# Projecting q once and spreading its rows through a DRAM scratch, in an attention kernel that feeds a gated feed-forward block

## The chip, the cores and the metric

The kernel runs on one core of a Trainium2 chip. A core has five engines with instruction streams of their own: TensorE (PE in the profile, with its weight loads as PEld), VectorE (DVE), ScalarE (ACT), GpSimd (POOL) and SyncE (SP), which here only issues DMA transfers. They meet through semaphores. The metric is the device time of one execution in microseconds (us). The profile is of one execution; its span runs from the first to the last instruction that it records.

## The reference

There are two blocks, in fp32. The first is attention with a polynomial sketch: every row of q and of k, 32 numbers long, is projected by S1 and S2 to 8 numbers each, and the outer product of the two results, 64 numbers, is its feature vector.

```python
def phi(x):                                   # x: (4, 4, 1088, 32)
    a = np.einsum('rd,bhsd->bhsr', S1, x)
    b = np.einsum('rd,bhsd->bhsr', S2, x)
    return np.einsum('bhsi,bhsj->bhsij', a, b).reshape(*x.shape[:-1], r * r)   # r = 8
q_p, k_p = phi(q), phi(k)
kv  = np.einsum('bhsf,bhsd->bhfd', k_p, v)
z   = np.sum(k_p, axis=2)
num = np.einsum('bhsf,bhfd->bhsd', q_p, kv)
den = np.einsum('bhsf,bhf->bhs', q_p, z)[..., None] + 1e-06
attn = num / den                              # then x = (4*1088, 4*32) = (4352, 128)
gate = 1.0 / (1.0 + np.exp(-(x @ w_gate)))    # w_gate, w_val: (128, 1536)
out  = (gate * (x @ w_val)) @ w_out           # w_out: (1536, 128)
```

The three weight matrices and S1, S2 arrive as 64-bit floats, so the kernel narrows them to fp32 itself with integer operations.

## The kernel before, in words

**The feed-forward block.** The 4352 tokens are cut into nine chunks, eight of 512 and one of 256. `xT` holds the tokens transposed. For a chunk the 1536 columns of the weights are taken in twelve blocks of 128. One *wave* (`w1`, matmuls at L293) computes gate and value of one block into a PSUM tile of the pool `psm`, which has two buffers; ACT takes the sigmoid of one half (L301, tile `sg`); `glu` (L311, VectorE) multiplies it by the other half and frees the PSUM tile; `w2` (L253) multiplies the result by the block of w_out and sums over the twelve blocks in the tile `moeout`. There are 102 waves.

**The attention block** handles one batch at a time, in two halves of q (n=0 with 512 rows of a head, n=1 with 576). `kps` (L379) projects k onto compact features, eight matmuls of 64 rows with the outputs of S1 and S2 of four heads side by side; VectorE transposes them (L389, `kab`), and `outer` (L400) forms the 64 features on POOL, or on VectorE for batch 0. `sum_z` (POOL, L494 to L499) sums them over the rows. `kv` (L460, L472) multiplies by v, `ndt` (L505) transposes. For q the feature dimension must lie on the partitions, so `ab` (L423) multiplies q twice by weights that already repeat the rows of S1 (`aps`) and of S2 (`bps`); ACT copies the first out (L433, `asb`), and VectorE multiplies the two (L442) into `qp`. An `r_group` is one such step: the second operand of one pair of heads together with the first operand of the next. Then `den` (L525) and `num` (L560) multiply `qp` by z and by kv; `invert` and `divide` on VectorE (L536 to L570) write the quotient into `xT`.

**What sets the order.** The order on PE, VectorE, ACT and POOL is written out by hand; each engine executes its instructions in that order. `slot(group, waves)` issues one piece of the attention of a batch and then some waves, each with the pending `glu` and `w2` in front of it. A wave is only issued if the attention has delivered its tokens. Only the DMA issues on SP may be moved by the scheduler; they too are executed in order.

**Narrowing.** In chunk 0 every wave also narrows weights: block j goes through four steps over several waves, POOL and ACT at first (L95, L99), then VectorE (L103, L107), then ACT and POOL (L111, L112), last VectorE (L115), which writes the fp32 block that the next wave uses. `load_w` fetches the 64-bit weights.

Of the kernel before, what the change touches and what calls it, by code (L numbers as in the profile page):

```python
# [8 lines left out]
F32 = mybir.dt.float32  # L9
# [5 lines left out]
MUL = ALU.mult  # L15

P = 128
# [3 lines left out]
def kernel(  # L21
# [12 lines left out]
    nc = tc.nc  # L34

    B, H, S, D = q.shape
    R = S1.shape[0]
# [6 lines left out]
    T = S // 32  # L44
# [7 lines left out]
    const = ctx.enter_context(tc.tile_pool(name="const", bufs=1))  # L52
    ld = ctx.enter_context(tc.tile_pool(name="ld", bufs=2))
    sbA = ctx.enter_context(tc.tile_pool(name="sbA", bufs=2))
    raw = ctx.enter_context(tc.tile_pool(name="raw", bufs=4))
    sbN = ctx.enter_context(tc.tile_pool(name="sbN", bufs=1))
    sbG = ctx.enter_context(tc.tile_pool(name="sbG", bufs=6))

    psm = ctx.enter_context(tc.tile_pool(name="psm", bufs=2, space=bass.MemoryType.PSUM))
    pso = ctx.enter_context(tc.tile_pool(name="pso", bufs=1, space=bass.MemoryType.PSUM))  # L60
    ps2 = ctx.enter_context(tc.tile_pool(name="ps2", bufs=1, space=bass.MemoryType.PSUM))
# [11 lines left out]
    TP = T // 2  # L73
    q_chk = [(0, 8), (8, TP - 8)]
# [245 lines left out]
    def glu():  # L320
        if moe["gate"] is not None:
            moe["gate"]()
            moe["gate"] = None
# [48 lines left out]
    KP, QP, ND, KAB, ASB, KVZ, KVD, RB = {}, {}, {}, {}, {}, {}, {}, {}  # L372

    def kps(b):
        t = ps2.tile([P, 2, 512], F32, tag="two", name="kps")
# [19 lines left out]
    def outer(b, pi, m0, m1, j0=0, j1=NJK, eng=nc.gpsimd):  # L395
# [8 lines left out]
            op=MUL,  # L404
        )

    def ab(a_of=None, b_of=None, pool_b=None):

        mm = []
        if a_of is not None:  # L410
            aps = psm.tile([P, 2, 512], F32, tag="wave", name="aps")
            mm.append((a_of, aps, sa))
        if b_of is not None:
            pool, tag = (ps2, "two") if pool_b is None else pool_b
            bps = pool.tile([P, 2, 512], F32, tag=tag, name="bps")
            mm.append((b_of, bps, sb))
        for c in range(2):
            for m in range(2):
                for (bb, pr, n), dst, sx in mm:
                    h = 2 * pr + m  # L420
                    rows = slice(32 * h, 32 * h + 32)
                    t0, tn = q_chk[n]
                    nc.tensor.matmul(  # L423
                        out=dst[64 * c : 64 * c + 64, m, : 32 * tn],
                        lhsT=sx[rows, :],
                        rhs=qT_of[bb][rows, t0 : t0 + tn, c, :],
                        start=True,
                        stop=True,
                    )
        if a_of is not None:  # L430
            w = 32 * q_chk[a_of[2]][1]
            ASB[a_of] = sbA.tile([P, 2, 288], F32, tag="asb", name="asb", bufs=3)
            nc.scalar.copy(out=ASB[a_of][:, :, :w], in_=aps[:, :, :w])  # L433
        if b_of is not None:

            def mult():
                bb, pr, n = b_of
                if bb not in QP:
                    QP[bb] = sbA.tile([P, H, TP * 32], F32, tag="qp", name="qp")
                t0, tn = q_chk[n]  # L440
                w = 32 * tn
                nc.vector.tensor_tensor(  # L442
                    out=QP[bb][:, 2 * pr : 2 * pr + 2, 32 * t0 : 32 * t0 + w],
                    in0=bps[:, :, :w],
                    in1=ASB[b_of][:, :, :w],
                    op=MUL,
                )

            return mult

    def kv(b, j_list, zsum=None):

# [67 lines left out]
    def den(b, n):  # L520
        t0, tn = q_chk[n]
        w = 32 * tn
        dps = ps1.tile([P, 512], F32, tag="one", name="dps")
        for h in range(H):
            nc.tensor.matmul(  # L525
                out=dps[32 * h : 32 * h + 32, :w],
                lhsT=zb[b % 2][:, h, :],
                rhs=QP[b][:, h, 32 * t0 : 32 * t0 + w],
                start=True,
                stop=True,  # L530
            )

        def invert():

            dT = sbA.tile([P, 9, 32], F32, tag="dT", name="dT")
            nc.vector.transpose(out=dT[:, :tn].rearrange("p t c -> p (t c)"), in_=dps[:, :w])  # L536
            rc = sbA.tile([P, 9, 2], F32, tag="rc", name="rc")
            nc.vector.tensor_scalar_add(rc[:, :tn], dT[:, :tn, :2], 1e-6)
            nc.vector.reciprocal(out=rc[:, :tn], in_=rc[:, :tn])

            rb = sbA.tile([P, 9, 2, 32], F32, tag="rb", name="rb")
            r0 = rc[:, :tn]
            nc.vector.transpose(
                out=rb[:, :tn].rearrange("p t c s -> p (t c s)"),
                in_=bass.AP(
                    tensor=r0.tensor, offset=r0.offset, ap=[list(r0.ap[0]), [1, 2 * tn], [0, 32]]
                ),
            )
# [106 lines left out]
    outer(1, 0, 0, 1)  # L655
    slot(lambda: r_group((1, 0, 0), None), 1)
    outer(1, 0, 1, 2)

    for b in range(1, B):
        more = b + 1 < B  # L660
# [5 lines left out]
        if b == 1:  # L666
            outer(b, 1, 0, 1)
        slot(lambda: r_group((b, 0, 1), (b, 1, 0)), wn)
        if b == 1:
            outer(b, 1, 1, 2)  # L670
# [11 lines left out]
        slot(lambda: den(b, 0)(), wn)  # L682

        def num0_den1():
            divide = num(b, 0)
            invert = den(b, 1)
            divide()
            invert()

        slot(num0_den1, wn)  # L690
        slot(lambda: num(b, 1)(), 1)
    slot(None, 10**3)


# [28 lines left out]
```

## Time and profile before

| | |
|---|---|
| time, median of 8 runs | 325.9 us (325.17 to 327.23) |
| the profiled execution | 325.5 us, of which its span is 323.7 us |
| granted TensorE clock | 0.998 of full speed |
| PE busy, 1562 matmul records | 311.5 us |
| VectorE, ACT, POOL busy | 141.4, 86.0, 48.5 us |
| DMA | 14.08 MB |

Every fp32 matmul shows as two records, so a wave has four. Ends of matmuls are modelled and consecutive ones overlap; the distance from start to start tells what one costs. In the lists of instructions the square bracket gives the idle time before an instruction and what ended it. SPq is the DMA queue of SyncE.

### The profile page before, as it was taken

To read this page: it belongs to the slowest core of one execution; us is meant where nothing else is said; L and a number is where in the kernel's file an instruction comes from. 1 tells how busy PE (TensorE), PEld (TensorE's weight loads), DVE (VectorE), ACT (ScalarE), POOL (GpSimd) and SP (SyncE) were. 2 spreads that over 40 slices of the span, in tenths; PEclk is the share of its full clock that TensorE was granted. 3 is DMA by queue.
4 is the path that set the end of the run, shared out by engine and by line. 5 is a ranking of instruction groups with operands and counts; after the bars stand their busy time and mean duration, and the time that the engine had idled before them with its cause. 6 is when DMAs were issued, how large, how long until landed. Compare 5 with 4: busy or idle time off the path is not lost.

```text
span 323.7 us, 3953 instructions
## 1 busy us (share of the span) xinstructions
PE 311.5 (96%) x1562; PEld 136.7 (42%) x1562; DVE 141.4 (44%) x248; ACT 86.0 (27%) x156; POOL 48.5 (15%) x53
## 2 busy tenths in 40 slices
PE   7779999899999999999999999999999999999995
PEld 2423433433344443333454434444444444444684
DVE  4887998455534333653313543242223222322321
ACT  2534544231233122122322221222222222222220
POOL 1433456674000290000000000000000000000000
PEclk9999999999999999999999999999999999999999
DMA  7999222130000200001000200010002000200021
GB/s 185 356 311 327 50 72 70 52 55 2 0 0 2 32 0 2 0 4 31 0 2 0 33 2 0 1 24 9 0 0 34 0 0 0 32 0 0 2 32 16
DMA packets 25586, 14.08 MB, mean 43 GB/s; under 512 B 19168, under 2 KB 22752, under 8 KB 25568
## 3 DMA queue, kind: packets, MB, share of 16 engines
q1 hardware_dynamic: 24736, 13.44, 15.9%
q10 hardware_dynamic: 832, 0.39, 0.6%
q8 instruction: 12, 0.20, 0.3%
q14 instruction: 6, 0.05, 0.1%
HBM read 11.60 MB, written 2.23 MB: 43 GB/s over the span
## 4 chain that ended last, share of the span: by engine, by line
PE 86%; DVE 4%; POOL 4%; DMA 3%; ACT 1%; issue 1%; SPq 0%; POOLq 0%; ACTq 0%; DVEq 0%
PE wave L293 52%; PE moeout L253 27%; DMA w_in<-in_moe_w_out_dram 2%; DMA k<-in_k_dram 1%; PE nps L560 1%; PE aps L423 1%; PE dps L525 1%; DVE w_sb L115 1%; POOL head L112 1%; DVE head L107 1%; POOL kp L400 1%; PE kvz L460 1%; POOL z L494 1%; PE bps L423 1%; PE kps L379 1%
## 5 line engine op out<-in xcount | busy, mean ns | idle before, releaser
L293 PE MATMUL wave<-xT,w_sb 128*128 128x512 f32 (+1 forms) x432 | 191.8, 570 | 3.4 <-DVE g L311 1.8
L311 DVE TENSOR_TENSOR g<-wave,sg 128x512 f32<-128x512 f32 x102 | 69.8, 685 | 122.3 <-ACT sg L301 122.0
L293 PEld LDWEIGHTS wave<-xT,w_sb 128*128 128x128 f32 x432 | 80.9, 190 | 99.0 <-issue 83.9
L301 ACT ACTIVATE sg<-wave 128x512 f32<-128x512 f32 x102 | 60.9, 597 | 213.1 <-PE wave L293 213.1
L253 PE MATMUL moeout<-g,w_sb 128*128 128x512 f32 (+1 forms) x216 | 105.9, 583 | 0.0
L253 PEld LDWEIGHTS moeout<-g,w_sb 128*128 128x128 f32 x216 | 38.2, 189 | 43.2 <-issue 38.7
L442 DVE TENSOR_TENSOR qp<-bps,asb 128x512 f32<-128x512 f32 (+1 forms) x16 | 11.5, 720 | 19.9 <-PE bps L423 14.6
L400 POOL TENSOR_TENSOR kp<-kab 128x576 f32<-128x576 f32 (+1 forms) x8 | 13.6, 1712 | 39.2 <-DVE kab L389 39.2
L112 POOL TENSOR_TENSOR head<-head,tail 128x384 int32<-128x384 int32 (+1 forms) x13 | 12.3, 947 | 24.3 <-DVE head L107 15.6
L423 PE MATMUL bps<-qT,s 32*64 32x256 f32 (+1 forms) x128 | 11.0, 412 | 0.4 <-DVE kab L389 0.4
L423 PE MATMUL aps<-qT,s 32*64 32x256 f32 (+1 forms) x128 | 11.3, 413 | 0.0
L433 ACT COPY asb<-aps 128x512 f32<-128x512 f32 (+1 forms) x16 | 9.7, 608 | 3.3 <-PE aps L423 1.9
L115 DVE SCALAR_TENSOR_TENSOR w_sb<-cap,head 128x384 f32<-128x384 f32 x12 | 9.8, 817 | 1.8 <-POOL head L112 1.8
L570 DVE TENSOR_TENSOR xT<-nps,rb 128x512 f32<-128x512 f32 (+1 forms) x8 | 5.8, 723 | 10.8 <-PE nps L560 10.7
L423 PEld LDWEIGHTS aps<-qT,s 32*64 32x64 f32 x128 | 3.6, 129 | 11.2 <-issue 6.6
L95 POOL TENSOR_SCALAR cap<-w_in 128x384 f32<-128x384 f32 x12 | 6.7, 566 | 7.5 <-DMA w_in<-in_moe_w_out_dram 7.5
L111 ACT ACTIVATE cap<-cap 128x384 f32<-128x384 f32 (+1 forms) x13 | 6.5, 499 | 4.6 <-DVE head L107 4.5
L226 PE MATMUL warm<-ones 128*128 128x512 f32 (+1 forms) x10 | 6.7, 800 | 0.9 <-DVE hm L232 0.9
L494 POOL TENSOR_TENSOR z<-kp 128x1024 f32<-128x1024 f32 x3 | 7.2, 2412 | 0.2
L263 DVE STREAM_TRANSPOSE o_sb<-moeout 128x512 f32<-128x512 f32 (+1 forms) x9 | 6.1, 677 | 2.5 <-PE moeout L253 2.5
L107 DVE SCALAR_TENSOR_TENSOR head<-cap,head 128x384 int32<-128x384 int32 (+1 forms) x13 | 6.9, 533 | 0.4
L99 ACT ACTIVATE tail<-w_in 128x384 int32<-128x384 uint32 x12 | 6.6, 558 | 1.6 <-DMA w_in<-in_moe_w_out_dram 1.6
(49 smaller groups left out, 97.1 us busy)
## 6 DMA issues: line engine op xcount, KB each, us to landing
v<-in_v_dram SPq DMA_DIRECT2D x16, 144.0 KB, 6.4
k<-in_k_dram SPq DMA_DIRECT2D x3, 544.0 KB, 5.3
q<-in_q_dram SPq DMA_DIRECT2D x3, 544.0 KB, 7.6
w_in<-in_moe_w_gate_dram SPq DMA_DIRECT2D x6, 256.0 KB, 5.5
w_in<-in_moe_w_val_dram SPq DMA_DIRECT2D x6, 256.0 KB, 6.1
w_in<-in_moe_w_out_dram SPq DMA_DIRECT2D x6, 256.0 KB, 6.2
out_dram<-o_sb SPq DMA_DIRECT2D x20, 64.0 KB, 2.0
k<-in_k_dram ACTq DMA_DIRECT2D x1, 288.0 KB, 3.7
```

Source lines behind the costliest of these rows:

```text
L107: nc.vector.scalar_tensor_tensor(out=head, in0=cap, scalar=-0x40000000, in1=head, op0=ALU.bitwise_and, op1=ALU.bitwise_or)
L112: nc.gpsimd.tensor_tensor(out=head, in0=head, in1=tail, op=ALU.add)
L115: nc.vector.scalar_tensor_tensor(out=out, in0=cap.bitcast(F32), scalar=1.265625 * 2.0**-30, in1=head.bitcast(F32), op0=ALU.is_ge, op1=MUL,)
L253: nc.tensor.matmul(out=moe["acc"][:, :tw], lhsT=w_sb[:, 2, j, :], rhs=g[:, jj, :tw], start=(j == 0), stop=(j == NJ - 1),)
L293: nc.tensor.matmul(out=wv[:, which, jj * tw : (jj + 1) * tw], lhsT=w_sb[:, which, j0 + jj, :], rhs=xT[:, t0 : t0 + tw], start=True, stop=True,
L301: nc.scalar.activation(out=sg, in_=wv[:, 0], func=ACTF.Sigmoid)
L311: nc.vector.tensor_tensor(out=g, in0=wv[:, 1], in1=sg, op=MUL)
L400: eng.tensor_tensor(out=o0.rearrange("p j m (i l) -> p (j m) i l", i=R), in0=bass.AP(tensor=a0.tensor, offset=a0.offset, ap=[pst] + jm + [ ...
L423: nc.tensor.matmul(out=dst[64 * c : 64 * c + 64, m, : 32 * tn], lhsT=sx[rows, :], rhs=qT_of[bb][rows, t0 : t0 + tn, c, :], start=True, sto ...
L433: nc.scalar.copy(out=ASB[a_of][:, :, :w], in_=aps[:, :, :w])
L442: nc.vector.tensor_tensor(out=QP[bb][:, 2 * pr : 2 * pr + 2, 32 * t0 : 32 * t0 + w], in0=bps[:, :, :w], in1=ASB[b_of][:, :, :w], op=MUL,)
L494: nc.gpsimd.tensor_tensor(out=z4, in0=kp[:, :, 1:5], in1=kp[:, :, 5:9], op=ALU.add)
```

## The change

For batch 0, n=0, everything stays. For all other halves the two products with repeated weights go. Instead `qcomp` projects q with the same compact weights as k, only reordered (`skq`): eight matmuls of 64 rows for a whole batch, or four for the half that is left of batch 0. ACT copies the result (`cq`) to SBUF. `spread` writes it to a scratch in DRAM, one transfer for each half and parity of the row blocks, and reads it back by four transfers for each half, in which the access pattern repeats each of eight rows eight times: once so that the rows of S1's projection are repeated (into `qp`), once those of S2's (into a new tile `bq`). `qmult` multiplies the two in place on VectorE, once for each half instead of once for each pair of heads.

The order is rewritten as well. `begin(b)` holds `kps`, `qcomp`, `spread` and the four `outer` of a batch; then come waves alone, `qmult` of the first half, `kv`, `ndt`, `qmult` of the second, `den`, `num`. Pieces of two batches no longer alternate. The layout of `qp` changes so that a half is contiguous; `kT` and `qT` get one buffer instead of two.

```diff
+    dram = ctx.enter_context(tc.tile_pool(name="dram", bufs=1, space=bass.MemoryType.DRAM))
...
-            kT_of[b] = sbA.tile([P, T, 32], F32, tag="kT", name="kT")
+            kT_of[b] = sbA.tile([P, T, 32], F32, tag="kT", name="kT", bufs=1)
...
-            qT_of[b] = sbA.tile([P, TP, 2, 32], F32, tag="qT", name="qT")
+            qT_of[b] = sbA.tile([P, TP, 2, 32], F32, tag="qT", name="qT", bufs=1)
...
+    def half(t, n):
+        t0, tn = q_chk[n]
+        o, w = 32 * H * t0, 32 * tn
+        return t[:, o : o + H * w].rearrange("p (h w) -> p h w", h=H)
...
+    def qcomp(b, ns, pool):
+        t = pool[0].tile([P, 2, 512], F32, tag=pool[1], name="cqps")
+        cq = sbA.tile([P, 2, 288], F32, tag="cq", name="cq", bufs=1)
+        for c in range(2):
+            for n in ns:
+                t0, tn = q_chk[n]
+                g = 2 * n + c
+                for pi in range(2):
+                    rows = slice(64 * pi, 64 * pi + 64)
+                    nc.tensor.matmul(
+                        out=t[32 * g : 32 * g + 32, pi, : 32 * tn],
+                        lhsT=skq[rows, :],
+                        rhs=qT_of[b][rows, t0 : t0 + tn, c, :],
+                        start=True,
+                        stop=True,
+                    )
+        w0, w1 = 32 * q_chk[0][1], 32 * q_chk[1][1]
+        if 0 in ns:
+            nc.scalar.copy(out=cq[:, :, :w0], in_=t[:, :, :w0])
+            nc.scalar.copy(out=cq[64:, :, w0:w1], in_=t[64:, :, w0:w1])
+        else:
+            nc.scalar.copy(out=cq[64:, :, :w1], in_=t[64:, :, :w1])
+        if b not in QP:
+            QP[b] = sbA.tile([P, H * TP * 32], F32, tag="qp", name="qp")
+        BQ[b] = sbA.tile([P, H * TP * 32], F32, tag="bq", name="bq", bufs=1)
+        return cq
+
+    def spread(b, ns, cq):
+        for n in ns:
+            w = 32 * q_chk[n][1]
+            d = dram.tile([2, 2, R, H, w], F32, tag=f"dq{n}", name="dq")
+            for c in range(2):
+                g = 2 * n + c
+                nc.sync.dma_start(
+                    out=d[c].rearrange("i r (m p) w -> (i r m) p w", m=2),
+                    in_=cq[32 * g : 32 * g + 32, :, :w],
+                )
+            for i, t in enumerate((QP[b], BQ[b])):
+                for c in range(2):
+                    d0 = d[c, i]
+                    rows = [[H * w, R], [0, R]] if i == 0 else [[0, R], [H * w, R]]
+                    nc.sync.dma_start(
+                        out=half(t, n)[64 * c : 64 * c + 64].rearrange("p h w -> p (h w)"),
+                        in_=bass.AP(
+                            tensor=d0.tensor, offset=d0.offset, ap=rows + [[1, H * w]]
+                        ),
+                    )
+
+    def qmult(b, n):
+        q0 = half(QP[b], n)
+        nc.vector.tensor_tensor(out=q0, in0=q0, in1=half(BQ[b], n), op=MUL)
...
-                rhs=QP[b][:, h, 32 * t0 : 32 * t0 + w],
+                rhs=half(QP[b], n)[:, 2 * (h % 2) + h // 2, :],
...
-                    rhs=QP[b][rows, h, 32 * t0 : 32 * t0 + w],
+                    rhs=half(QP[b], n)[rows, 2 * (h % 2) + h // 2, :],
...
-    def r_group(a_of, b_of):
-        m = ab(a_of, b_of)
-        if m is not None:
-            m()
...
+    skq = const.tile([P, 2, R, 2], F32, tag="skq")
+    nc.gpsimd.tensor_copy(out=skq, in_=sk.rearrange("p m n r -> p n r m"))
+    skq = skq.rearrange("p n r m -> p (n r m)")
...
-    slot(lambda: r_group((0, 0, 1), None), 1)
-    slot(lambda: r_group((0, 1, 1), (0, 0, 1)), 1)
-    slot(lambda: r_group(None, (0, 1, 1)), 1)
+    def begin(b):
+        glu()
+        kps(b)
+        cq[b] = qcomp(b, (0, 1), (psm, "wave"))
+        spread(b, (0, 1), cq[b])
+        for pi in range(2):
+            for m in range(2):
+                outer(b, pi, m, m + 1)
...
+    def q01():
+        spread(0, (1,), qcomp(0, (1,), (ps2, "two")))
+
+    slot(q01, 4)
+    turn_k(1)
+    slot(None, 2)
+    turn_q(1, 0)
+    turn_q(1, 1)
+    slot(None, 1)
+    qmult(0, 1)
     slot(lambda: den(0, 1)(), 1)
     slot(lambda: num(0, 1)(), 1)
-    turn_k(1)
-    slot(None, 1)
-    turn_q(1, 0)
-    slot(lambda: kps(1), 1)
-    outer(1, 0, 0, 1)
-    slot(lambda: r_group((1, 0, 0), None), 1)
-    outer(1, 0, 1, 2)
     for b in range(1, B):
-        wn = 1 if b == 1 else 2
+        wn = 2 if b == 1 else 3
         load_batch(b + 1)
-        turn_q(b, 1)
-        slot(lambda: r_group((b, 1, 0), (b, 0, 0)), wn)
...
-        zs = sum_z(b)
-        slot(lambda: r_group((b, 1, 1), (b, 0, 1)), wn)
-        turn_k(b + 1)
-        slot(lambda: kv(b, [1, 2, 3, 4, 5, 6, 7, 8, 0], zs), wn)
-        if more:
-            slot(lambda: kps(b + 1), wn)
-            for pi in range(2):
-                outer(b + 1, pi, 0, 2)
-        turn_q(b + 1, 0)
-        slot(lambda: ndt(b), wn)
-        slot(lambda: r_group((b + 1, 0, 0) if more else None, (b, 1, 1)), wn)
...
+        slot(lambda: begin(b), wn)
+        zs = sum_z(b)
+        slot(None, 2 * wn - 1)
+        qmult(b, 0)
+        slot(lambda: kv(b, [1, 2, 3, 4, 5, 6, 7, 8, 0], zs), wn)
+        slot(lambda: ndt(b), wn - 1)
+        qmult(b, 1)
+        slot(lambda: den(b, 0)(), wn)
+        slot(lambda: num0_den1(b), wn)
+        slot(lambda: num(b, 1)(), 1)
+        turn_k(b + 1)
+        slot(None, 1)
+        turn_q(b + 1, 0)
+        turn_q(b + 1, 1)
+        slot(None, 1)
```

More of the change, by code (lines that the diff above doesn't have):

```diff
@@ L370, in turn_q @@
         )
-    KP, QP, ND, KAB, ASB, KVZ, KVD, RB = {}, {}, {}, {}, {}, {}, {}, {}
+    KP, QP, BQ, ND, KAB, ASB, KVZ, KVD, RB = {}, {}, {}, {}, {}, {}, {}, {}, {}
     def kps(b):
@@ L431, in ab @@
             w = 32 * q_chk[a_of[2]][1]
-            ASB[a_of] = sbA.tile([P, 2, 288], F32, tag="asb", name="asb", bufs=3)
+            ASB[a_of] = sbA.tile([P, 2, 256], F32, tag="asb", name="asb", bufs=2)
             nc.scalar.copy(out=ASB[a_of][:, :, :w], in_=aps[:, :, :w])
@@ L438, in mult @@
                 if bb not in QP:
-                    QP[bb] = sbA.tile([P, H, TP * 32], F32, tag="qp", name="qp")
+                    QP[bb] = sbA.tile([P, H * TP * 32], F32, tag="qp", name="qp")
                 t0, tn = q_chk[n]
@@ L442, in mult @@
                 nc.vector.tensor_tensor(
-                    out=QP[bb][:, 2 * pr : 2 * pr + 2, 32 * t0 : 32 * t0 + w],
+                    out=half(QP[bb], n).rearrange("p (m c) w -> p c m w", m=2)[:, pr],
                     in0=bps[:, :, :w],
@@ L645, with num0_den1 @@
     slot(None, 1)
-    slot(lambda: r_group((0, 0, 1), None), 1)
-    slot(lambda: r_group((0, 1, 1), (0, 0, 1)), 1)
-    slot(lambda: r_group(None, (0, 1, 1)), 1)
+    cq = {}
+    def begin(b):
[6 more added lines that the diff above has]
+                outer(b, pi, m, m + 1)
+    def num0_den1(b):
+        divide = num(b, 0)
+        invert = den(b, 1)
+        divide()
+        invert()
@@ L649 @@
+    def q01():
[7 more added lines that the diff above has]
+    qmult(0, 1)
     slot(lambda: den(0, 1)(), 1)
     slot(lambda: num(0, 1)(), 1)
-    turn_k(1)
-    slot(None, 1)
-    turn_q(1, 0)
-    slot(lambda: kps(1), 1)
-    outer(1, 0, 0, 1)
-    slot(lambda: r_group((1, 0, 0), None), 1)
-    outer(1, 0, 1, 2)
     for b in range(1, B):
-        more = b + 1 < B
-        wn = 1 if b == 1 else 2
+        wn = 2 if b == 1 else 3
@@ L663 @@
         load_batch(b + 1)
-        turn_q(b, 1)
-        slot(lambda: r_group((b, 1, 0), (b, 0, 0)), wn)
[L666 to L670, printed above, removed]
-        zs = sum_z(b)
-        slot(lambda: r_group((b, 1, 1), (b, 0, 1)), wn)
-        turn_k(b + 1)
-        slot(lambda: kv(b, [1, 2, 3, 4, 5, 6, 7, 8, 0], zs), wn)
-        if more:
-            slot(lambda: kps(b + 1), wn)
-            for pi in range(2):
-                outer(b + 1, pi, 0, 2)
@@ L679 @@
-        turn_q(b + 1, 0)
-        slot(lambda: ndt(b), wn)
-        slot(lambda: r_group((b + 1, 0, 0) if more else None, (b, 1, 1)), wn)
[L682 to L691, printed above, removed]
+        slot(lambda: begin(b), wn)
+        zs = sum_z(b)
+        slot(None, 2 * wn - 1)
+        qmult(b, 0)
+        slot(lambda: kv(b, [1, 2, 3, 4, 5, 6, 7, 8, 0], zs), wn)
```

## The prediction, made before the changed kernel was run

> **What bounds the kernel now.** First the page's busy shares and its chain.
>
> ```profile
> PE 311.5 (96%) x1562; PEld 136.7 (42%) x1562; DVE 141.4 (44%) x248; ACT 86.0 (27%) x156; POOL 48.5 (15%) x53
> ...
> PE 86%; DVE 4%; POOL 4%; DMA 3%; ACT 1%; issue 1%; SPq 0%; POOLq 0%; ACTq 0%; DVEq 0%
> ```
>
> TensorE sets the time. A busy share is an average, so next the busy time by stage, the columns being core time, then PE, PEld, DVE, ACT, POOL.
>
> ```profile
> 18.50:26.90 8.40, 6.32 (x34) 2.07 (x34) 6.63 (x12) 4.59 (x9) 4.50 (x6) 1.00 1.06 284
> 26.90:50.75 23.85, 23.51 (x115) 8.49 (x115) 21.07 (x40) 10.87 (x22) 10.60 (x14) 1.00 0.40 120
> 50.75:63.65 12.90, 11.63 (x130) 4.83 (x131) 7.98 (x12) 3.74 (x7) 9.87 (x9) 1.00 0.19 57
> ...
> 110.00:200.00 90.00, 89.27 (x446) 36.67 (x443) 35.77 (x64) 21.00 (x37) 9.42 (x6) 1.00 0.04 7
> ```
>
> PE idles 2.08, 0.34, 1.27 and 0.73 us here, 4.4 in all, and not at all from 63.65 to 110. Removed PE work is therefore worth its full time after 63 us. From 26.9 to 50.75, though, VectorE is busy for 21.07 of 23.85 us, so what PE saves there is only kept if VectorE keeps up.
>
> What does one attention insert cost? From the timeline of PE (start, length):
>
> ```profile
> 84.06 1.88 PE L293 MATMUL wave<-xT,w_sb 128*128 128x512 f32 x4
> 85.86 0.43 PE L423 MATMUL aps<-qT,s 32*64 32x256 f32 x1
> ...
> 86.48 1.13 PE L253 MATMUL moeout<-g,w_sb 128*128 128x512 f32 x2
> 87.45 1.88 PE L293 MATMUL wave<-xT,w_sb 128*128 128x512 f32 x4
> 89.16 1.02 PE L253 MATMUL moeout<-g,w_sb 128*128 128x512 f32 x2
> 90.02 1.88 PE L293 MATMUL wave<-xT,w_sb 128*128 128x512 f32 x4
> ```
>
> A wave and its w2 alone take 90.02 - 87.45 = 2.57 us. With an r_group between them it is 87.45 - 84.06 = 3.39. The insert costs 0.82: 0.62 for the group and about 0.19 for the two changes of shape. The groups with 288 columns cost 0.87 (93.46 - 90.02 = 3.44 around the one at 91.83).
>
> Last, the chain that narrows the weights in chunk 0, on VectorE and POOL:
>
> ```profile
> 20.46 0.87 DVE L115 SCALAR_TENSOR_TENSOR w_sb<-cap,head 128x384 f32<-128x384 f32 x1 [0.49 <-POOL head L112]
> 21.26 0.35 DVE L103 TENSOR_SCALAR head<-cap 128x384 int32<-128x384 int32 x1
> 21.64 0.56 DVE L107 SCALAR_TENSOR_TENSOR head<-cap,head 128x384 int32<-128x384 int32 x1
> 22.12 0.68 DVE L311 TENSOR_TENSOR g<-wave,sg 128x512 f32<-128x512 f32 x1
> 23.41 0.88 DVE L115 SCALAR_TENSOR_TENSOR w_sb<-cap,head 128x384 f32<-128x384 f32 x1 [0.61 <-POOL head L112]
> ```
>
> ```profile
> 22.38 1.00 POOL L112 TENSOR_TENSOR head<-head,tail 128x384 int32<-128x384 int32 x1 [1.46 <-DVE head L107]
> 23.34 0.53 POOL L95 TENSOR_SCALAR cap<-w_in 128x384 f32<-128x384 f32 x1
> ```
>
> Each wave needs the column narrowed one round earlier. A round is L115, L103, L107, then 1.29 us until POOL has made head: 23.41 - 20.46 = 2.95 us when VectorE has only one glu to fill the gap. Today a wave takes 3.4 us here, which hides it.
>
> [...] L115 takes 0.87 us where cap follows head on POOL and 0.55 elsewhere[...]. [...] The scratch reads have a slowest dimension of 8[...]; nothing in this trace shows such a transfer.
>
> **The change, part by part.**
>
> *PE.* Sixteen r_groups go: three of batch 0 (n=1), thirteen for batches 1 to 3. Four have 256 columns, twelve have 288: 4 x 0.82 + 12 x 0.87 = 13.7 us. Four qcomp calls come. For batches 1 to 3, eight 64-row matmuls are put directly behind kps, which has the same shape and takes 0.65 (65.46 to 66.11): 3 x 0.65. For batch 0 it is an insert of its own, 0.84. Net: 13.7 - 2.8 = **-10.9 us**. The order of waves, w2, den, num, ndt and kv keeps its counts.
>
> *Idle that goes.* Wave 2 today waits 1.75 us for a PSUM buffer that aps took; three other short waits (1.3 us) on the copy of aps are of the same kind; and kv waits 1.27 for zs on POOL. In the changed order qcomp of batch 0 takes the other pool, and begin calls glu first, so its buffer comes free a wave early. **-4.4 us.**
>
> *kv's operands move.* kps and outer of batch 1 go into begin, after num(0,1). POOL then needs four outers (1.2 each) and sum_z (5.1), about 10 us behind kab. Between kps and the zs part of kv stand two inserts, five waves and the kv matmuls: about 14 us. Hidden with some 3 us to spare, 6 more for batches 2 and 3, which have eight waves.
>
> *VectorE and ACT.* Fourteen mults go (6 x 0.68 + 8 x 0.76 = 10.2 us) and seven qmults come[...]. On ACT fourteen asb copies (8.5) become seven cq copies (about 3). Neither engine bounds after 63 us (VectorE 21.5 busy in the 46.4 from 63.65), so nothing there. skq's copy falls into POOL's 7.5 us wait for w_in. Single buffers for kT and qT cost nothing: their readers, kps and qcomp, are waves earlier.
>
> *Chunk 0 is where it costs.* I walk the after order of VectorE with the durations above. Wave 2 can start at 21.3 (column 1 done), not 22.86. Columns 2 to 5 then end every 2.95 us, 24.2 to 33.1. PE would need 2.58, so waves 3 to 6 lose 0.35 + 3 x 0.37 = 1.5, and wave 2 loses 0.25. turn_k(1) (1.24) stands between L107 and glu, partly inside POOL's 1.29; wave 7 loses 0.5, wave 8 0.37. Both turn_q(1) (1.3) stand before glu 7, the second moved forward from 49.5. So VectorE is through its L107 at 43.25 and qmult(0,1) ends at 44.5. den(0,1) is the next PE instruction behind wave 8, which ends at 41.0: 3.5 us of PE idle, and w2, wave 9 and all else queue behind den. Sum: **+6.1 us**, in a stage which today has next to none. Afterwards VectorE has the slack of den and num to catch up.
>
> *Scratch.* SP issues the two writes of batch 0 after w_in of the last columns (today at 25.7), so near 27, behind a full queue; landed by about 32.5. k of batch 2 (0.54 MB) goes in between. The four reads are 1.18 MB. How fast? An unloaded 544 KB load shows
>
> ```profile
> GB/s 0 0 0 0 0 0 174 174 261 218 326 392 392 413 326 109 0 0 0 0 0 0 41 0 0 0 0 0 0 0 0 0 0 0 0 0 0 0 0 0
> ...
> q<-in_q_dram SPq DMA_DIRECT2D x1, 544.0 KB, 3.3
> ```
>
> 400 GB/s on 16 engines. [...] I take 200[...]. Landed near 40, against 43.25 for qmult. Batch 1: by the same walk wave 10 begins at 49.4 (den 0.65, w2 0.86 twice, wave 9 1.72 and num 0.65 behind the 44.5), and kps and qcomp end at 52.5; then ACT's copy, writes from 53.2 on, landed 2 us later (out stores of 64 KB land in 2.0), first half there at 61.4, second at 67.5, against qmults at about 63.4 and 72.8. Batches 2 and 3 have three waves more. SP's other load, out stores of 64 KB, falls behind the reads and is on no path. So scratch is hidden, at 0; its cover is the waves, and a late read would hold VectorE, then den on PE.
>
> *Sum:* -10.9 - 4.4 + 6.1 = -9.2 us. Span 323.7 to 314.5; the profiled execution's 325.5 becomes 316.3. The median of the runs, 325.9, is 0.4 above it: **316.7 us**.
>
> **Rivals.**
>
> *The narrowing does not bind.* If VectorE finds POOL done, as it does today, the 6.1 us stay away: 325.9 - 15.3 = 310.6. For it: the L115 of the middle waves take 0.55. Against it: those waves have attention work to fill the gap. 0.13, half-way cases included.
>
> *PE waits longer and cools.* [...] this trace shows only the start, where six warm matmuls took 4.95 us against 0.46 each later. The wait at den is 3.5. [...] 0.18.
>
> *The scratch reads are late: slower.* At a rate R, batch 0's reads land at 33.2 + 1180/R us (R in GB/s, 1180 KB[...]) against 43.25, and batch 1's at 56.1 + 2230/R against 72.8. At 100 GB/s they are 1.8 and 5.6 late, at 92 it is 2.8 and 7.5. It outweighs the gain from about 95 GB/s down; at 80 the time is 333. Against it stand 400 GB/s for long rows here[...]. 0.06.
>
> *Nothing changes,* gains and stalls cancelling: 0.03.
>
> **How the numbers follow.** My sum has 0.60, with 314.5 to 319 as its own range (the den wait between 1.5 and 5.5 us). Cooling adds the stretch to 321; the narrowing's half-way cases go down to 312.5. Range 312.5 to 321. A measurement of this kernel can tell about 0.2% from no change. Faster 0.90, same 0.03, slower 0.07.
>
> **What would show it.** PE busy near 300; only the first eight aps and eight bps of batch 0 left, and cqps stretches of 0.65 us; waves of chunk 0 spaced near 2.95 us; a wait of PE's den on VectorE's qmult of 2 to 5 us near 41 to 45; spacing of 2.57 or 3.4 with no gaps after 66 us; scratch reads landing some 8 us after issue at most. It is wrong if VectorE waits for a DMA at a qmult, if kv waits for POOL, or if PE idles after 70 us.

## The result, and the profile after

The changed kernel takes 321.43 us in the median of 11 runs (316.87 to 323.73), the kernel before 325.69 us (32 runs on the same chips). The ratio is 0.9798, with a 95% interval from 0.977 to 0.9826. Applied to the 325.9 us of the prediction it gives 319.3 us (318.4 to 320.2), against 316.7 forecast. The ratio leaves out executions over 1.5% above the kernel's fastest, five here, while the median holds them; the experiments make it likely that with this kernel they belong to what the change does. The profiled execution took 317.59 us, the second fastest of the eleven; its span is 315.8.

First the busy shares and the chain on the page of the kernel after:

```profile
PE 303.1 (96%) x1394; PEld 136.5 (43%) x1394; DVE 140.9 (45%) x241; ACT 81.4 (26%) x149; POOL 49.3 (16%) x58
...
PE 85%; DMA 12%; SPq 1%; DVE 1%; issue 0%; POOL 0%; ACT 0%; POOLq 0%
```

PE lost 8.4 us of busy time and 168 records. The chain before held 3% of DMA; now it holds 12%: part of the span hangs on transfers. Where? The busy time by stage of the same kernel (core time, then PE, PEld, DVE, ACT, POOL, the granted clock, the DMA share and GB/s), from wave 1 on:

```profile
17.72:38.67 20.95, 19.46 (x49) 7.30 (x50) 17.18 (x30) 11.15 (x22) 10.49 (x14) 1.00 0.87 243
38.67:52.61 13.94, 9.53 (x38) 3.29 (x37) 9.55 (x19) 3.53 (x7) 3.48 (x4) 0.76 0.68 154
52.61:76.00 23.39, 23.39 (x162) 10.68 (x161) 10.68 (x18) 6.15 (x12) 11.03 (x9) 1.00 0.44 121
76.00:110.00 34.00, 34.00 (x150) 13.86 (x149) 18.00 (x30) 7.83 (x15) 8.52 (x7) 1.00 0.16 44
```

All idle time of PE in these stages, 1.49 + 4.41 us, lies ahead of 52.61, and the clock falls to 0.76 in one stage. From 52.61 to 110 PE has no gap in this execution. The timeline of PE shows both (start, length, what; idle time before it in the bracket):

```profile
23.59 1.98 PE L295 MATMUL wave<-xT,w_sb 128*128 128x512 f32 x4
...
26.56 1.98 PE L295 MATMUL wave<-xT,w_sb 128*128 128x512 f32 x4
...
29.52 1.98 PE L295 MATMUL wave<-xT,w_sb 128*128 128x512 f32 x4
...
44.96 1.19 PE L587 MATMUL dps<-qp,zb 128*32 128x288 f32 x8 [4.41 <-DVE qp L511]
46.07 2.08 PE L255 MATMUL moeout<-g,w_sb 128*128 128x512 f32 x2
47.94 3.13 PE L295 MATMUL wave<-xT,w_sb 128*128 128x512 f32 x4
51.00 0.72 PE L622 MATMUL nps<-qp,nd 64*32 64x288 f32 x16
```

The waves of chunk 0 stand 2.97 and 2.96 us apart, where PE needs 2.57. Then `den(0,1)` waits 4.41 us for VectorE, and what follows runs at half speed, with a granted clock of 0.50 over den and w2 and 0.59 over the wave: from start to start den takes 1.11 us (0.62 at full clock), w2 1.87 (0.97) and the wave 3.06 (1.81). That is 0.49 + 0.90 + 1.25 = 2.6 us on top of the wait. From `num` at 51.00 on all is normal again.

The timeline of VectorE has what kept it: once a round POOL, as before the change, and new the scratch reads at two of the seven qmults.

```profile
22.66 0.88 DVE L117 SCALAR_TENSOR_TENSOR w_sb<-cap,head 128x384 f32<-128x384 f32 x1 [0.61 <-POOL head L114]
...
41.96 0.56 DVE L109 SCALAR_TENSOR_TENSOR head<-cap,head 128x384 int32<-128x384 int32 x1
43.49 1.42 DVE L511 TENSOR_TENSOR qp<-qp,bq 128x1152 f32<-128x1152 f32 x1 [0.97 <-DMA bq<-dq]
...
69.23 1.22 DVE L511 TENSOR_TENSOR qp<-qp,bq 128x1024 f32<-128x1024 f32 x1 [1.76 <-DMA bq<-dq]
```

And the chain of work in that stretch (start, length, what):

```profile
26.23 3.99 DMA dq<-cq
...
32.29 11.18 DMA bq<-dq
...
43.49 1.43 DVE qp L511
...
44.96 1.19 PE dps L587 x8
```

The last read of batch 0 lands at 43.46, 11.2 us after its issue, where the prediction had 40. Right behind the four reads SP issued more loads (its timeline):

```profile
31.66 1.20 SPq L502 DMA_DIRECT2D bq<-dq  x2
32.96 0.41 SPq L177 DMA_DIRECT2D q<-in_q_dram  x1
33.42 1.85 SPq L191 DMA_DIRECT2D v<-in_v_dram  x4
37.46 0.35 SPq L177 DMA_DIRECT2D k<-in_k_dram  x1
40.65 0.35 SPq L177 DMA_DIRECT2D q<-in_q_dram  x1
```

DMA from 20 to 50 us in 40 slices of 0.75 us, first the busy tenths of the 16 DMA engines, then GB/s:

```profile
DMA  9999999989998752554596999999998999855542
GB/s 253 220 218 190 255 332 281 332 309 188 341 186 208 293 221 67 184 160 123 129 200 180 262 263 194 186 206 156 110 122 255 396 293 221 126 87 181 209 197 99
```

What the transfers do when little else runs is to be seen at batch 1, whose eight reads are issued from 58.8 to 64.2. DMA from 56 to 70 us in 40 slices of 0.35 us, in the same two lines:

```profile
DMA  0000253669005555445534544635449795373545
GB/s 0 0 0 0 73 114 99 141 158 225 20 0 159 217 152 176 94 94 129 140 94 140 152 105 164 176 117 176 105 167 234 176 251 129 155 196 105 211 119 184
```

While the reads run alone about half of the engines' time is used, at some 150 GB/s.

### The profile page after: what moved, and what is told of

Read it like the earlier page. It is cut to its first block, busy times and chain, and to the rows that moved or that the text cites. A ratio compares the mean times of both kernels' runs of the same rounds, so it can differ in the third digit from the quotient of the medians.

```text
span 315.8 us, 3677 instructions
## 1 busy us (share of the span) xinstructions
PE 303.1 (96%) x1394; PEld 136.5 (43%) x1394; DVE 140.9 (45%) x241; ACT 81.4 (26%) x149; POOL 49.3 (16%) x58
## 4 chain that ended last, share of the span: by engine, by line
PE 85%; DMA 12%; SPq 1%; DVE 1%; issue 0%; POOL 0%; ACT 0%; POOLq 0%
PE wave L295 52%; PE moeout L255 27%; DMA bq<-dq 4%; DMA q<-in_q_dram 3%; DMA w_in<-in_moe_w_val_dram 2%; DMA w_in<-in_moe_w_gate_dram 2%; PE dps L587 2%; PE nps L622 1%; DMA dq<-cq 1%; PE kvz L522 1%; PE kps L381 1%; SPq L502 1%; PE cqps L470 0%; DVE qp L511 0%; SPq L177 0%
## 5 line engine op out<-in xcount | busy, mean ns | idle before, releaser
L295 PEld LDWEIGHTS wave<-xT,w_sb 128*128 128x128 f32 x432 | 82.1, 191 | 97.7 <-issue 87.9
L255 PEld LDWEIGHTS moeout<-g,w_sb 128*128 128x128 f32 x216 | 39.4, 191 | 45.0 <-issue 37.8
L402 POOL TENSOR_TENSOR kp<-kab 128x576 f32<-128x576 f32 x12 | 14.1, 1201 | 88.2 <-DVE kab L391 88.2
L117 DVE SCALAR_TENSOR_TENSOR w_sb<-cap,head 128x384 f32<-128x384 f32 x12 | 9.7, 811 | 3.9 <-POOL head L114 3.9
L587 PE MATMUL dps<-qp,zb 128*32 128x256 f32 (+1 forms) x64 | 5.8, 438 | 4.7 <-DVE qp L511 4.4
L511 DVE TENSOR_TENSOR qp<-qp,bq 128x1152 f32<-128x1152 f32 (+1 forms) x7 | 9.1, 1297 | 2.7 <-DMA bq<-dq 2.7
L97 POOL TENSOR_SCALAR cap<-w_in 128x384 f32<-128x384 f32 x12 | 6.7, 563 | 5.0 <-DMA w_in<-in_moe_w_out_dram 5.0
L109 DVE SCALAR_TENSOR_TENSOR head<-cap,head 128x384 int32<-128x384 int32 (+1 forms) x13 | 6.9, 533 | 0.4
L522 PE MATMUL kvz<-kp,v 128*32 128x64 f32 (+1 forms) x288 | 6.7, 222 | 0.1
L522 PEld LDWEIGHTS kvz<-kp,v 128*32 128x32 f32 (+1 forms) x288 | 5.3, 109 | 3.5 <-issue 2.7
L622 PE MATMUL nps<-qp,nd 64*32 64x256 f32 (+1 forms) x128 | 6.1, 401 | 0.7 <-issue 0.7
```

The source lines that it names most:

```text
L117: nc.vector.scalar_tensor_tensor(out=out, in0=cap.bitcast(F32), scalar=1.265625 * 2.0**-30, in1=head.bitcast(F32), op0=ALU.is_ge, op1=MUL,)
L255: nc.tensor.matmul(out=moe["acc"][:, :tw], lhsT=w_sb[:, 2, j, :], rhs=g[:, jj, :tw], start=(j == 0), stop=(j == NJ - 1),)
L295: nc.tensor.matmul(out=wv[:, which, jj * tw : (jj + 1) * tw], lhsT=w_sb[:, which, j0 + jj, :], rhs=xT[:, t0 : t0 + tw], start=True, stop=True,
L402: eng.tensor_tensor(out=o0.rearrange("p j m (i l) -> p (j m) i l", i=R), in0=bass.AP(tensor=a0.tensor, offset=a0.offset, ap=[pst] + jm + [ ...
L511: nc.vector.tensor_tensor(out=q0, in0=q0, in1=half(BQ[b], n), op=MUL)
L522: nc.tensor.matmul(out=kvz[32 * h : 32 * h + 32, F * which : F * which + F], lhsT=v_t[b][:kr, h, j, :] if which == 0 else ones[:kr, :], rh ...
```

## The experiments

All are edits of the changed kernel unless said otherwise. Each ratio is to the kernel before on the same chip, whose median there lies between 325.6 and 326.6 us. Edits shift the line numbers a little; in experiments 6 and 10 den is L598 and qmult L522.

**1. Batch 0 without the scratch** (`e1_b0_old_way`). The second half of batch 0 goes back to three r_groups, with den and num straight behind them and so ahead of the transposes of batch 1; batches 1 to 3 keep the scratch. (The definition of `r_group` and the width of `asb`, which come back too, are left out here.)

```diff
-    slot(q01, 4)
+    slot(lambda: r_group((0, 0, 1), None), 1)
+    slot(lambda: r_group((0, 1, 1), (0, 0, 1)), 1)
+    slot(lambda: r_group(None, (0, 1, 1)), 1)
+    slot(lambda: den(0, 1)(), 1)
+    slot(lambda: num(0, 1)(), 1)
     turn_k(1)
...
-    slot(None, 1)
-    qmult(0, 1)
-    slot(lambda: den(0, 1)(), 1)
-    slot(lambda: num(0, 1)(), 1)
+    slot(None, 2)
```

> Batch 0, n=1, goes back to the three old r_groups; batches 1 to 3 keep qcomp and the scratch. Theory (PE's saving is real everywhere, and what is lost is the wait of den(0,1) for qmult, 4.5 us, with 2.6 us of half clock behind it): both go, three inserts of 0.87 come back for one of 0.84, and about 1 us of the narrowing's waits is filled by them. Profiled execution 317.6 - 7.1 + 1.8 - 1.0 = 311.3 us, about 0.955 to 0.962 of before, with no cold stretch in the clock and little scatter. Rival (the scratch traffic of batches 1 to 3 costs as well, and causes the scatter): no better than 0.975, scatter as now.

Measured: 315.53 us, ratio 0.9672 (0.9646 to 0.9698). The wait at den and the half clock are gone, although PE executes about 1.7 us more (three inserts for one qcomp). But a wait shows further on that the profile after did not have, in PE's timeline:

```profile
75.68 1.88 PE L295 MATMUL wave<-xT,w_sb 128*128 128x512 f32 x4
79.14 1.13 PE L255 MATMUL moeout<-g,w_sb 128*128 128x512 f32 x2 [1.58 <-DVE g L313]
```

w2 waits for glu, which is queued on VectorE behind `qmult(1,1)`, and that one waits for its scratch read:

```profile
DVE qp L511 <- DMA bq<-dq: 5.3, 2, 2.8
```

(In the view of waits: us in total, times, longest.) So batch 1 comes to its second half before the reads do. This wait is 1.6 of the 4.0 us by which the profiled execution, 315.29, missed the expected 311.3; 1.8 more are an old wait that comes back with the r_groups, that of wave 2 for a PSUM buffer (at 22.70).

**2. Two more waves ahead of den** (`e2_den_two_waves_later`).

```diff
-    slot(None, 1)
+    slot(None, 3)
     qmult(0, 1)
```

> qmult, den and num of batch 0, n=1, stand two waves later (waves 10 to 12 of chunk 0), all else as in the changed kernel. Theory (the wait is a meeting of late reads, narrowing and both turn_q just before qmult): reads have landed and VectorE has caught up in the two waves, so den waits 0.5 to 1.5 us and the clock stays up: 311 to 313 us, about 0.957 to 0.963 of before. Rival (VectorE is behind PE at any wave of chunk 0, by 3 us or more): den waits as long as now, 316 us or more.

Measured: 318.0 us, 0.9754 (0.9708 to 0.98), between the two theories. VectorE no longer waits for the read, yet den still waits for VectorE, and PE stays warm in the profiled execution (PE's timeline):

```profile
41.51 1.13 PE L255 MATMUL moeout<-g,w_sb 128*128 128x512 f32 x2 [0.71 <-DVE g L313]
...
49.35 0.69 PE L587 MATMUL dps<-qp,zb 128*32 128x288 f32 x8 [2.42 <-DVE qp L511]
49.98 1.12 PE L255 MATMUL moeout<-g,w_sb 128*128 128x512 f32 x2
```

Of the wait of 4.41 us, 0.97 was the late read. Another 0.71 has only moved: w2 at 41.51, which in the changed kernel stands behind den, now waits for a glu in VectorE's row. That leaves 2.42 at den and some 0.3 that VectorE caught up in two waves. The warm clock is not the rule either: of the six executions two, at 320.5 us, show a mean clock of 0.989, that of the profiled execution of the changed kernel, and the others 0.994 to 1.0. Again w2 waits later, 1.48 us at 84.93, behind `qmult(1,1)`.

**3. The wait filled with idle matmuls** (`e3_filled_wait`). Five matmuls of 512 columns, whose result nobody reads, keep PE busy ahead of den.

```diff
     qmult(0, 1)
+    cover()
     slot(lambda: den(0, 1)(), 1)
```

> Five idle matmuls of 512 columns (4.3 us) into a free PSUM tile ahead of den(0,1), nothing else changed. Theory [...]: den starts at the same time, but dps, w2 and wave 9 behind it run at full clock: 2.6 us less, near 315 us, and the scatter of the runs, 316.9 to 323.7, shrinks to 1% or so. Rival (the clock fell for another reason, or the scatter is the reads' landing): no change in the mean, scatter as now.

Measured: 317.97 us, 0.975 (0.9725 to 0.9776), with a spread from 317.74 to 318.54. PE's timeline:

```profile
41.18 4.47 PE L732 MATMUL cover<-ones 128*128 128x512 f32 x10
46.43 0.69 PE L587 MATMUL dps<-qp,zb 128*32 128x288 f32 x8 [0.77 <-DVE qp L511]
47.05 1.12 PE L255 MATMUL moeout<-g,w_sb 128*128 128x512 f32 x2
```

The waves behind den run at full clock, as the theory has it, but the expected 315 was missed by 3 us: w2 waits later, 1.13 us at 81.65, and the read came later too, so that den starts 1.5 us later than in the changed kernel. Even so `num` follows at 49.82 against 51.00. By the medians, work that nobody needs makes the kernel 3.5 us faster (the profiled executions are level, 317.8 and 317.6, and the intervals of the two ratios just touch), and its runs agree within 0.25% where those of the changed kernel differ by 2%: the half clock is a cost of its own, and a source of the spread.

**4. VectorE's other work out of the way** (`e4_turn_q_later`). `turn_q(1,0)` and `turn_q(1,1)`, 1.36 us together ahead of qmult(0,1), move behind den and num.

```diff
-    slot(None, 2)
-    turn_q(1, 0)
-    turn_q(1, 1)
-    slot(None, 1)
+    slot(None, 3)
     qmult(0, 1)
     slot(lambda: den(0, 1)(), 1)
+    turn_q(1, 0)
     slot(lambda: num(0, 1)(), 1)
+    turn_q(1, 1)
```

> Both turn_q(1) move behind qmult(0,1) and num(0,1). Theory (VectorE and the reads are late together, the reads by 1 us more): VectorE reaches qmult 1.3 us earlier and waits 2 us for bq instead of 1, den starts at most 0.4 us earlier, time as the changed kernel within 1 us. Rival (VectorE alone sets it, as predicted blind): den starts 1.3 us earlier and the clock stays up, 313 to 314 us.

Measured: 321.63 us, 0.9831 (0.979 to 0.9871). Den waits 4.17 us all the same, as qmult now waits for its read. And a second cold stretch appears (PE's timeline):

```profile
45.49 1.19 PE L587 MATMUL dps<-qp,zb 128*32 128x288 f32 x8 [4.17 <-DVE qp L511]
...
85.58 2.08 PE L255 MATMUL moeout<-g,w_sb 128*128 128x512 f32 x2 [2.75 <-DVE g L313]
```

The 2.08 us of w2 at 85.58 are half clock again; the read of batch 1's second half held VectorE for 3.9 us there. VectorE and the read end at nearly the same time in chunk 0; taking work from one of them does not help.

**5. The best version: 1, and qmult(b,1) behind den(b,0)** (`e5_qmult_later`). Nothing needs `qmult(b,1)` before `den(b,1)`, so the read gets two or three more waves.

```diff
-        qmult(b, 1)
         slot(lambda: den(b, 0)(), wn)
+        qmult(b, 1)
         slot(lambda: num0_den1(b), wn)
```

> On top of e1_b0_old_way: qmult(b,1) stands behind den(b,0) instead of before it, two waves later for batch 1 and three for the others. Theory (in e1 the 1.6 us of PE idle at 79 us is w2 behind a glu behind qmult(1,1), which waits 2.8 us for bq): that wait goes, PE is without a gap from 53 us to the end, 313.5 to 314.2 us where e1 had 315.5, about 0.961 of before. Rival (two waves are not enough, or the wait comes back at den(1,1)): as e1, 0.967.

Measured: **314.08 us** (313.67 to 314.81), 0.9623 (0.9603 to 0.9643), faster than both kernels. Its stages, to be set beside those of the changed kernel:

```profile
38.67:52.61 13.94, 13.22 (x61) 5.27 (x60) 12.60 (x24) 7.44 (x15) 6.34 (x8) 1.00 0.27 82
...
76.00:110.00 34.00, 34.00 (x144) 14.10 (x144) 16.66 (x27) 7.96 (x14) 9.65 (x8) 1.00 0.25 61
```

PE idles 0.72 us in the second stage where it idled 4.41, at full clock, and the gap of experiment 1 near 79 is closed.

**6. Reads with a slowest dimension of 16** (`e6_sixteen_engines`). The scratch is laid out so that the operand `qp` of a half is one read whose slowest dimension is 16; the reads of `bq` keep 8. The writes become four transfers of 16 partitions per half.

```diff
-                    out=d[c].rearrange("i r (m p) w -> (i r m) p w", m=2),
-                    in_=cq[32 * g : 32 * g + 32, :, :w],
+                        out=d[i, c].rearrange("r (m p) w -> (r m) p w", m=2),
+                        in_=cq[32 * g + 16 * i : 32 * g + 16 * i + 16, :, :w],
...
+                if i == 0:
+                    d0 = d[0, 0]
+                    nc.sync.dma_start(
+                        out=half(t, n).rearrange("p h w -> p (h w)"),
+                        in_=bass.AP(
+                            tensor=d0.tensor, offset=d0.offset,
+                            ap=[[H * w, 2 * R], [0, R], [1, H * w]],
+                        ),
+                    )
+                    continue
...
-                    d0 = d[c, i]
+                    d0 = d[i, c]
```

> The changed kernel with its scratch in the order projection, parity, row: the reads into qp become one transfer of 128 partitions whose slowest dimension is 16, those into bq stay at 8; writes are four of 16 partitions instead of two of 32 per half, and in the scheduler's order k of batch 2 now follows the reads of batch 0. Theory [...]: while qp is read the DMA engines are busy 9 tenths and move some 300 GB/s, while bq is read 5 tenths and 150 as now; bq's last landing comes 2 to 4 us earlier in batch 1, and VectorE's waits for bq there go. Rival (the scratch's memory limits, not the engines): qp's reads stay near 150 GB/s whatever the count of engines.

Measured: 315.82 us, 0.9674 (0.9634 to 0.9713). DMA from 48 to 75 us, in slices of 0.675 us:

```profile
DMA  9987552000000222408997335545200069999388
GB/s 186 152 162 251 206 206 97 0 0 24 0 12 0 49 49 49 83 21 194 328 240 154 100 115 146 121 127 116 72 3 0 0 171 355 273 170 198 139 197 242
```

Both kinds of read stand side by side. The `qp` reads of batch 1, issued at 58.94 and 68.49, fill nine tenths of the engines, with some 260 GB/s over three slices and up to 328 and 355 in one; the `bq` reads behind the first of them fill five tenths, with 100 to 146. What was expected of VectorE in batch 1 failed: it still waits 1.48 and 1.09 us for `bq` there. In chunk 0 qmult(0,1) no longer waits for a read; the wait at den is VectorE's alone, 3.31 us, and still cools PE (PE's timeline):

```profile
44.20 1.19 PE L598 MATMUL dps<-qp,zb 128*32 128x288 f32 x8 [3.31 <-DVE qp L522]
45.31 2.08 PE L255 MATMUL moeout<-g,w_sb 128*128 128x512 f32 x2
```

This run also changed the order of transfers on SP (k of batch 2 now follows the reads of batch 0), so not all of its gain is the layout's.

**7. What one insert costs** (`e7_idle_groups`). Experiment 5 with eight idle groups put between waves of batches 2 and 3; nobody reads their result. Each has four matmuls of 288 columns, like an r_group with one operand; one with both has eight.

```diff
-        slot(None, 2 * wn - 1)
+        if b == 1:
+            slot(None, 2 * wn - 1)
+        else:
+            for _ in range(4):
+                slot(lambda: idle_group(b), 1)
+            slot(None, 1)
```

> On top of e5: eight extra groups of four 32-row matmuls of 288 columns, with no reader, one before each of four waves in batches 2 and 3, where PE has no idle time. Theory (an insert costs 0.82 to 0.87 us, the price used for the removed r_groups): 6.6 to 7.0 us more than e5. Rival (TensorE overlaps such a group with its neighbours and the gain of the change was in its order): under 3 us more.

Measured: 320.72 us, 6.64 more than experiment 5 on the same chip: 0.83 us for each insert. PE's timeline has two waves 106.02 - 102.60 = 3.42 us apart, where experiment 5 has 2.57:

```profile
102.60 1.88 PE L295 MATMUL wave<-xT,w_sb 128*128 128x512 f32 x4
104.41 0.71 PE L748 MATMUL idle<-qT,s 32*64 32x288 f32 x8
...
106.02 1.88 PE L295 MATMUL wave<-xT,w_sb 128*128 128x512 f32 x4
```

**8. Narrowing one block further ahead** (`e8_narrow_ahead`, one execution).

```diff
-            narrow_w(j0 + 2, 1)
-            narrow_w(j0 + 2, 2)
+            narrow_w(j0 + 3, 1)
+            narrow_w(j0 + 3, 2)
```

> The changed kernel with steps two and three of narrowing one wave further ahead of step four, nothing else. Theory (the waves of chunk 0 are 2.95 us apart because L117 waits 1.29 us for POOL's head within the round): waves 3 to 6 are 2.58 to 2.65 apart, VectorE waits for no head, and den's wait grows by what is saved, since the reads land when they did: the time stays as it is within the scatter. Rival (VectorE's own work or PE sets 2.95): the spacing stays.

Measured: 319.03 us. The waves stand 2.80 us apart (28.23, 31.03, 33.83), half-way between 2.95 and what PE needs. In these rounds VectorE does not wait for POOL's head any more, but its instructions got longer (its timeline):

```profile
27.01 1.08 DVE L117 SCALAR_TENSOR_TENSOR w_sb<-cap,head 128x384 f32<-128x384 f32 x1
28.01 0.68 DVE L105 TENSOR_SCALAR head<-cap 128x384 int32<-128x384 int32 x1
```

In the changed kernel they took 0.88 and 0.35 in the same rounds. The wait turned into lengthening: from 17.7 to 38.7 us VectorE is busy for 20.63 of 21.00 us here, against 17.18 of 20.95 in the changed kernel, and POOL's fourteen instructions there take 12.07 us for 10.49. That each slows the other is likely from this and not shown. And den waits 4.82 us, since the reads do not land sooner because the waves do (qmult(0,1) starts at 45.56, after 1.59 us of waiting for its read).

**9. qmult(b,1) later, and nothing else** (`e9_late_qmult_alone`): the edit of experiment 5 on the changed kernel itself, to see whether the second cold stretch makes its spread.

> Edit: the changed kernel with qmult(b, 1) moved behind the slot of den(b, 0), nothing else. What is asked: the changed kernel's median is 321.4 us where its profiled execution had 317.6, and its executions scatter by 2 per cent. Theory A (two cold stretches): in the slower executions the reads of batch 1's second half land after VectorE reaches qmult(1, 1), glu and w2 queue behind it, TensorE waits again and runs at half clock a second time. Then moving this qmult behind den takes the second stretch away: median 316.5 to 318.5, scatter within 1 per cent, a den wait near 4.4 us in chunk 0 with one cold stretch as before, no idle time of PE from 53 to 110. Theory B (the scatter comes from the first stretch alone, cold for longer or shorter): median stays at 320 to 322 with the same scatter.

Measured: 319.13 us (317.78 to 320.59), 0.9782 (0.9749 to 0.9815). The median is 2.3 us lower than the changed kernel's and no run lies above 320.6, which speaks for theory A. So does the mean clock on record for each execution. It is 0.983 in the profiled execution of experiment 4, which has two cold stretches, 0.984 in that kernel's two slowest and in four executions of the changed kernel above 321.6 us, and never under 0.988 here. But the intervals of the two ratios overlap, the clock differs by 0.005 and more between executions of the kernel before as well, and the median is above A's range. The profiled execution had a longer wait in chunk 0 (its chain of work):

```profile
33.51 12.73 DMA bq<-dq
...
47.67 1.19 PE dps L587 x8
```

Writes and reads of the same size took 4.69 and 12.73 us here, 3.99 and 11.18 in the profile after, and den waited 6.27 us. So both stretches are likely to make the spread; in what shares was not settled.

**10. The scratch for all halves, mended** (`e10_all_scratch`): the layout of experiment 6, the two more waves of 2 and the late qmult of 5.

> Edit: the scratch laid out so that the reads of qp are one transfer of slowest dimension 16 (as in the run with sixteen engines), slot(None, 1) ahead of qmult(0, 1) made slot(None, 3), and qmult(b, 1) behind the slot of den(b, 0). All halves but the first still go through the scratch. Theory: the den wait of 3.3 us becomes 1 to 2 us and stays under what cools TensorE, and no later wait arises; 317.6 - 2.6 (half clock) - 2 to 3 (wait) gives 312 to 314, level with or below the 314.1 of the version that does batch 0 in the old way. Rival: the two more waves ahead of den only move the lateness of VectorE, and den waits over 3 us and cools: 316 to 318.

Measured: 316.18 us (314.66 to 316.52), 0.9684 (0.9656 to 0.9711): the rival's range, though den's wait is under the 3 us that the rival named. No read holds qmult(0,1), and den waits 2.43 us, as in experiment 2. But here PE cooled (its timeline):

```profile
49.53 0.69 PE L598 MATMUL dps<-qp,zb 128*32 128x288 f32 x8 [2.43 <-DVE qp L522]
50.16 1.44 PE L255 MATMUL moeout<-g,w_sb 128*128 128x512 f32 x2
51.39 3.30 PE L295 MATMUL wave<-xT,w_sb 128*128 128x512 f32 x4
```

In VectorE's timeline its rounds of that stretch stand 2.6 us apart (L117 at 44.16 and 46.78), as the waves do, so more waves ahead of den don't let VectorE catch up; of the 3.31 us of experiment 6, 0.71 stands at an earlier w2 here too (at 41.69). L117, L105, L109 and a glu stand between a wave's weights and qmult. Doing batch 0's second half in the old way (314.08) remains better than sending it through the scratch.

## Why the prediction was right or wrong

**PE, -10.9 us: right.** Busy time fell by 8.4, and 2.6 of half clock had been added: 11.0. Experiment 7 puts 0.83 us on an insert of one operand, where 0.82 to 0.87 was read off for inserts of two. The 11.0 is good to about 1.5 us, since a part of the waits in chunk 0 lies within PE's busy time (below).

**Idle that goes, -4.4: right.** None of these waits is left in the profile after; kv does not wait for POOL.

**Chunk 0, +6.1: right in kind, a little small.** The waves stand 2.96 us apart for 2.95 worked out. From the start of wave 2 (20.73) to that of wave 8 (38.67) are 17.94 us where six steps of 2.57 are 15.4: 2.5 lost, for 2.4 worked out. PE's idle time from wave 1 on shows only 1.49, as the ends of matmuls are modelled. The wait at den was 4.41 for 3.5. Without the 0.97 for which VectorE waited for the read it is 3.44, but that this fits so well is luck: VectorE was through its L109 at 42.52, 0.7 before the time worked out, and wave 8 ended at 40.55, 0.45 before. With the 0.41 ahead of wave 2 that makes 7.3 us from start to start; 5.9 of them show as idle time. The time of a qmult, which no trace of before shows, was the author's estimate; it took 1.22 us for 1024 columns and 1.42 for the 1152 of qmult(0,1).

**"So scratch is hidden, at 0": wrong.** The step that failed is the rate of 200 GB/s that the reads were to have to themselves: the author's estimate, since no trace of before shows such a read. Batch 0's writes landed at 30.2, before the 32.5 estimated; its reads landed at 43.46 instead of 40. From 30.5 to 43.3 us the 16 engines moved about 2.3 MB (the slices of that stretch, 177 GB/s in the mean), while the reads are 1.18 MB: the other half is the loads of q, v and k that SP issues from 32.96 on. That these held the reads up is read from the bytes; no run leaves them out. The walk counted the load ahead of the reads and none behind them. Where reads run alone, at batch 1, they move some 150 GB/s and use about half of the 16 engines' time; in experiment 6 it is five tenths with a slowest dimension of 8, nine with 16. The first half of batch 1 was there 12.9 us after its writes began, not 8.2. The error costs little in the profiled execution, 0.97 us at den; in experiments 1 to 4 the same lateness at qmult(1,1) costs PE 1.1 to 2.75. The rival "slower" was nearer than its chance says. It put the point where lateness outweighs the gain at 95 GB/s, and batch 0's reads came in at about 94 (an estimate: 1180 KB between 30.91, where SP has issued the first of them, and 43.46). It cost little there because the writes had landed 2.3 us before their time, which is luck, and because batch 1's reads moved some 150.

**The half clock: right in kind, wrong in place.** It stood in a rival with a chance of 0.18. After what wait the clock falls, and what that costs, no trace of before shows, so both were the author's estimate. Here it fell after a wait of 4.41 us, at the den for which the sum itself had put 3.5, and the stretch cost 2.6 us. (The "six warm matmuls" of the prediction are six records, so three matmuls.) No single length of wait divides these runs: waits of 2.42 us (experiment 2) and 2.43 (experiment 10) left PE warm in one case and cold in the other, and by the clocks on record executions of experiment 2 itself differ, from 0.989 to 1.0. But waits of 2.43, 2.75 and 3.31 us cooled PE, all shorter than the 3.5 of the sum, so a margin is needed.

**Working the sum again** with chunk 0 and the half clock as the profile has them: -10.9 - 4.4 + 5.9 + 2.6 = -6.8 us. From the start of wave 1 to the end the profiles have 305.2 before and 298.1 after, -7.1. Busy and idle time add up to the span, so this is bookkeeping and no test of each term. A further 0.8 us of the difference of the spans lies ahead of wave 1, which the change does not explain. So that the profiled execution, 317.6 us, came within 1.3 of the 316.3 worked out is in part luck: the sum lacks a loss of 2.6, the half clock, and a gain of 0.8, the shorter start.

**The range** of 312.5 to 321.0 holds the 319.3 by the ratio and misses the median of all runs by 0.4 us. What it lacked is the case of two cold stretches in one execution, which experiment 4 shows. The prediction's own sign of failure, VectorE waiting for a DMA at a qmult, came true; PE idling after 70 did in experiments 1 to 4, not in the profile after.

## What to carry to other kernels

Work taken off the engine that sets the time pays its start-to-start price, but in a stage where another engine is nearly as busy the saving turns into a wait, and on TensorE a wait (2.43 us and more in these runs) may be paid a second time as half clock: fill it, or leave the stage's work as it was. When a transfer is to be hidden, count what its queue issues behind it as well as ahead of it, and put its consumer as late as the one who reads the result allows. Here the change is best applied only to the batches where TensorE alone is the bound (314.1 us in experiment 5, against 319.1 in experiment 9, which differs from it only in batch 0).

## What the runs showed of the hardware

- Repeated-row reads from DRAM with a slowest dimension of 8 used about five tenths of the 16 DMA engines' time at some 100 to 150 GB/s; with 16, nine tenths at some 260 GB/s, up to 355 (experiment 6).
- In the profiled executions, half clock after waits of 2.43 us (experiment 10), 2.75 and 4.17 (4), 3.31 (6), 4.41 (the kernel after), 4.82 (8) and 6.27 (9), none after one of 2.42 (2); one such stretch cost 2.6 us in the kernel after.
- L117 took 0.54 us where POOL was through `cap` (L97) before it began, 0.87 where POOL goes on to narrow the next block beside it (`cap`), 1.38 beside `outer` (0.94 to 1.52 in the kernel before, where the prediction has 0.55 elsewhere) and 1.08 in experiment 8; after the same wait of 0.60 for POOL, but with no `cap` left to do, it took 0.56 (experiment 2). The median of L105 went from 0.35 in the kernel after to 0.68 in experiment 8. So the chain of narrowing could not simply be overlapped away: 2.95 us a round became 2.80 in experiment 8.
